# A new instruction order, small guard operations on other engines, and four loads in flight instead of eight in a fused attention and soft-MoE kernel

## The chip, the cores and the metric

One core of one Trainium2 chip runs the whole program. The metric is the device time of one execution in microseconds (us). Five engines work beside each other, each on its own queue in order: PE (TensorE, with its weight loads shown as PEld), DVE (VectorE), ACT (ScalarE), POOL (GpSimd) and SP (SyncE, which issues all DMAs here). They wait for one another by semaphores.

## The reference

Two attentions in a row (32 packed queries over 576 rows, then 576 queries over the 32 packed rows), and a soft mixture of experts over all 4608 rows of the result:

```python
def sm_attn(qq, kk, vv):
    s = scale * np.matmul(qq, kk.transpose(0, 1, 3, 2))
    a = np.exp(s - np.max(s, axis=-1, keepdims=True))
    a = a / (np.sum(a, axis=-1, keepdims=True) + 1e-09)
    return np.matmul(a, vv)
p_packed = sm_attn(p, k, v)                 # 8 batches, 8 heads, 32 x 64
out = sm_attn(q, p_packed, p_packed)        # 8 batches, 8 heads, 576 x 64
...
logits = x @ phi                            # x: 4608 x 512, phi: 512 x 32
d = softmax over the 4608 rows of logits    # per slot, 1e-09 in its sum too
slot_input = d.T @ x                        # 32 slots
h = np.maximum(slot_input[e] @ w1[e], 0.0)  # 8 experts, 4 slots each
slot_out[e] = h @ w2[e]
c = softmax over the 32 slots of logits
return c @ slot_out
```

All data are float32. w1 and w2 together are 33.6 MB, and q, k and v 28.3 MB.

## The kernel before

**Steps.** The attention runs in 8 steps i of 2 batches and 4 heads each; two steps make a round dd (0 to 3). A step's parts have short names, and each is one Python function `f_<name>`: `kt` transposes k on DVE (L393), `s1` scores the packed queries (PE, L409), `mx1`/`e1` the row maxima (DVE, L422) and the exponentials with their row sums `rz` (ACT, L425), `ap`/`apc` transpose them (PE, L442, and a copy), `m` multiplies by v (PE, L464), `rz` (L474) adds the guard 1e-9 to the sums, inverts them and multiplies them by the 0/1 mask `rm` (three DVE instructions, L476, L477, L479), `ppa`/`pp` scale the products with that (ACT L488, DVE L493), `pt`/`ptc` transpose them, `mp`/`mm` multiply by phi. For the second attention `qp`/`qc` transpose q (PE L555, and a copy), `s2` scores (PE, L581), `mx2`/`sb`/`e2` subtract the maxima and take exponentials (DVE L602 and L612, ACT L641), `z2` sums (POOL as a tree, L649 to L655, or DVE, L646), `rc` adds the guard (DVE, L659) and inverts (L660), `n2` normalises (POOL or DVE, L664), `a2p`/`a2c` transpose the result (PE L673). Per round, `lg` makes the logits (PE L697), `f1` to `f6` take the running maximum over all rows and the exponentials (`f3`: three or four DVE instructions, L714 to L723; `f4`: PE, L731 and L739), and `gr`, `rt`, `gt`, `rb`, `gs`, `sa` accumulate the slots' inputs (PE L801, L823, L860). `f_w` (L833) multiplies a tile of ones into a PSUM bank that nobody reads.

**What sets the order.** `ORDER` is a string of such tokens, worked off from left to right: `qp.1.4@6` is part 4 of `qp` in step 1 into PSUM bank 6, and `:a`, `:v`, `:p` name the engine of a copy. Each engine gets its instructions in this order. Matmuls in float32 show in the trace as two records each.

**Loads.** All loads are issued by SP in the order of the list `loads`: p, and then k, q and v of each step, in pieces of 590 KB, then the weights in 33 chunks, of 1 MB but for two halves. They go into one ring in SBUF; `pump` issues the next load in program order once `release` has freed its place (for q and v after their last PE use, for k after its DVE transposes). The framework gives the loads 8 semaphores in turn, so each load also waits for the one eight places ahead. `PLACE` says of the first 21 weight chunks which go to the ring (`r`), which into work tiles that come free late (`0` to `5`, opened by the tokens `late`), and which into the tile a2 (`x`, opened by `lx`).

**After the steps.** The last `gs.3` and one DVE addition (L1012) complete the slots' inputs. Then PE consumes the weight chunks (`layer1a`, L948, 16 chunks of w1; then layer 2, L1002 and L1054), the last 12 loads following into the ring as chunks of w1 are consumed, and at the end the rows of the output are made (L1114), copied and stored.

Of the kernel before, what the change touches and what calls it, by code (L numbers as in the profile page):

```python
# [24 lines left out]
ppa.0.1 ppa.0.0 pp.0.1 kt.1.2 kt.1.3 s1.1.0@4 pp.0.0 kt.1.1 pt.0.0 ptc.0.1:v s1.1.1 ptc.0.0:v mp.0.0
mx1.1.0 mm.0.0:a s2.0.0@0 e1.1.1 s2.0.1 e1.1.0 rz.1.0 kt.2.0 ap.1.0@7 qp.1.4@6 ap.1.2@5 qc.1.4:a
apc.1.0:v qp.1.1@4 qp.1.3@3 apc.1.2:a mx2.0.2 qp.1.0@7 qc.1.1:a qc.1.3:a qp.1.2@6 qc.1.0:a qp.1.5@3
kt.2.3 qc.1.2:a ap.1.1@4 qc.1.5:a kt.2.2 m.1.0@6 apc.1.1:v sb.0.2 m.1.1 m.1.2 kt.2.1 e2.0.0 s1.2.0@0
ppa.1.0 s1.2.1 z2.0.0:p ppa.1.1 pp.1.0 pp.1.1 pt.1.0 mx1.2.0 ptc.1.1:a ptc.1.0:a mp.1.0 kt.3.1
e1.2.0 kt.3.0 mm.1.0:a e1.2.1 s2.1.0@5 rc.0.0 rz.2.0 n2.0.0:p s2.1.1 kt.3.2 kt.3.3 qp.2.2@0 qp.2.1@1  # L30
mx2.1.2 qp.2.5@2 qc.2.1:a qp.2.4@3 ap.2.0@1 qc.2.5:a ap.2.2@4 qc.2.2:v apc.2.0:a qp.2.3@2 qc.2.4:v
qp.2.0@1 sb.1.2 qc.2.3:a a2p.0.1@0 qc.2.0:a ap.2.1@3 a2p.0.0@2 a2c.0.1:a apc.2.1:v e2.1.0 m.2.0@5
apc.2.2:v m.2.1 a2c.0.0:a z2.1.0:p m.2.2 s1.3.0@0 ppa.2.0 ppa.2.1 pp.2.0 pp.2.1 pt.2.0 a2p.0.2@4
kt.4.0 ptc.2.1:a s1.3.1 ptc.2.0:a a2c.0.2:a kt.4.2 rc.1.0 lg.0.0@4 kt.4.3 mp.2.0 n2.1.0:p mm.2.0:a
mx1.3.0 s2.2.0@5 s2.2.1 kt.4.1 e1.3.0 e1.3.1 mx2.2.2 qp.3.1@3 sb.2.2 ap.3.1@2 qc.3.1:a ap.3.2@1
apc.3.1:a qp.3.5@0 a2p.1.1@2 apc.3.2:v qc.3.5:a qp.3.4@3 qp.3.0@7 rz.3.0 qc.3.4:a a2c.1.1:a qp.3.2@0
e2.2.0 ap.3.0@3 qp.3.3@2 apc.3.0:v a2p.1.0@1 qc.3.0:a z2.2.0:v m.3.0@5 a2c.1.0:a qc.3.2:a m.3.1
rc.2.0 m.3.2 qc.3.3:v n2.2.0:p a2p.1.2@7 ppa.3.1 ppa.3.0 pp.3.1 s1.4.0@0 pp.3.0 a2c.1.2:v s1.4.1
kt.5.2 a2p.2.0@7 kt.5.0 lg.0.1 a2c.2.0:v pt.3.0 f1.0.0 a2p.2.1@7 ptc.3.0:a kt.5.3 ptc.3.1:a f2.0.0
a2c.2.1:a mp.3.0 f3.0.0 a2p.2.2@7 mm.3.0:a mx1.4.0 a2c.2.2:a f4.0.0 f5.0.0 s2.3.0@5 fd.0.0 e1.4.1  # L40
kt.5.1 s2.3.1 e1.4.0 f6.0.0 mx2.3.2 ap.4.0@3 ap.4.2@2 ap.4.1@1 apc.4.2:a qp.4.2@0 sb.3.2 apc.4.1:a
qp.4.1@2 qc.4.1:a qp.4.3@1 qp.4.4@2 qc.4.3:a fl.0.0 gr.0.0@5 qc.4.2:v e2.3.0 gz.0.0 apc.4.0:v
qc.4.4:a lg.1.0@7 rt.0.1:v rt.0.0:a z2.3.0:p rz.4.0 s1.5.0@0 gt.0.0 s1.5.1 kt.6.2 rb.0.0 mx1.5.0
gs.0.0 qp.4.0@4 sa.0.0 e1.5.0 qc.4.0:v m.4.0@5 kt.6.1 e1.5.1 m.4.1 rc.3.0 m.4.2 n2.3.0:v ap.5.1@0
ppa.4.1 ap.5.0@1 ppa.4.0 ap.5.2@2 apc.5.1:v apc.5.0:a a2p.3.2@3 apc.5.2:a pp.4.1 a2p.3.1@4 a2c.3.2:v
a2p.3.0@0 a2c.3.1:a m.5.0@1 kt.6.0 a2c.3.0:a kt.6.3 m.5.1 pp.4.0 m.5.2 rz.5.0 pt.4.0 ppa.5.1 lg.1.1
ppa.5.0 pp.5.1 ptc.4.1:a pp.5.0 ptc.4.0:a qp.4.5@0 f1.1.0 pt.5.0 qc.4.5:a f2.1.0 mp.4.0 ptc.5.1:v
ptc.5.0:a f3.1.0 mm.4.0:a mp.5.0 mm.5.0:v f4.1.0 s1.6.0@0 f5.1.0 s1.6.1 kt.7.0 fd.1.0 s2.4.0@4
mx1.6.0 s2.4.1 kt.7.2 e1.6.1 f6.1.0 mx2.4.2 e1.6.0 ap.6.1@3 rz.6.0 qp.5.0@2 apc.6.1:v qp.5.2@1
qc.5.0:a gz.1.0 ap.6.0@0 qc.5.2:a sb.4.2 qp.5.1@2 ap.6.2@3 apc.6.0:a qp.5.4@1 qc.5.1:a qp.5.3@0  # L50
qc.5.4:a apc.6.2:a fl.1.0 gr.1.0@1 e2.4.0 kt.7.3 kt.7.1 qc.5.3:a z2.4.0:p s1.7.0@4 rt.1.1:v rt.1.0:a
gt.1.0 s1.7.1 late.0.0 late.1.0 rb.1.0 gs.1.0 mx1.7.0 qp.5.5@0 qc.5.5:a sa.1.0 rc.4.0 e1.7.1 m.6.0@2
n2.4.0:p m.6.1 e1.7.0 m.6.2 rz.7.0 ap.7.0@7 ppa.6.0 s2.5.0@4 ppa.6.1 apc.7.0:a pp.6.0 pp.6.1
a2p.4.1@7 a2p.4.0@0 a2c.4.1:v pt.6.0 a2c.4.0:a s2.5.1 ptc.6.1:v ptc.6.0:a qp.6.2@7 mx2.5.2 mp.6.0
qc.6.2:a qp.6.5@0 mm.6.0:a qp.6.0@1 qc.6.5:a sb.5.2 qp.6.1@2 qp.6.3@3 qc.6.0:a qp.6.4@0 ap.7.1@7
qc.6.1:a qc.6.3:a a2p.4.2@1 qc.6.4:v ap.7.2@2 e2.5.0 s2.6.0@3 apc.7.2:v a2c.4.2:a z2.5.0:p s2.6.1
apc.7.1:a qp.7.3@7 mx2.6.2 qp.7.1@6 qp.7.2@2 qc.7.3:a qp.7.4@1 lg.2.0@0 qc.7.1:a qc.7.2:a sb.6.2
m.7.0@6 qc.7.4:a m.7.1 late.2.0 rc.5.0 e2.6.0 m.7.2 n2.5.0:v qp.7.5@5 ppa.7.1 ppa.7.0 qp.7.0@4
qc.7.5:a pp.7.1 a2p.5.0@3 pp.7.0 qc.7.0:v pt.7.0 a2c.5.0:a a2p.5.2@5 ptc.7.1:a ptc.7.0:v a2p.5.1@1
z2.6.0:v s2.7.0@2 a2c.5.1:a s2.7.1 late.3.0 rc.6.0 a2c.5.2:v n2.6.0:p mp.7.0 mx2.7.2 lg.2.1 mm.7.0:a  # L60
# [1093 lines left out]
```

## Time and profile before

| | |
|---|---|
| device time, median of 3 runs | 215.29 us (215.11 to 216.77) |
| the profiled execution's own time | 214.82 us |
| its span, first to last instruction | 212.9 us |
| PE busy (2769 matmul records) | 174.0 us, 82% |
| DVE busy | 135.4 us, 64% |
| ACT busy | 82.0 us, 39% |
| POOL busy | 34.9 us, 16% |
| mean granted clock of TensorE | 0.917 of full speed |
| HBM traffic | 62.46 MB read, 9.44 MB written |
| chain that ended last, by engine | PE 41%, DVE 20%, DMA 13%, ACT 11%, issue 4%, POOL 2% |

The times of the trace count from the span's start. A granted clock of 1.00 is 2.4 GHz and 0.50 is 1.2 GHz; a value between them is a stretch that had both. The chain is followed back from the last instruction: at each step to what released it, or to the instruction before it on its engine.

### The profile page before, as it was taken

Reading aid. Unit: us, or ns where it says so; the run is one execution under the profiler, and the core shown is the slowest. Engines: PE = TensorE matmul, PEld = TensorE weight load, DVE = VectorE, ACT = ScalarE, POOL = GpSimd, SP = SyncE. Lnnn points to the kernel's source line nnn. Section 1 sums busy time; section 2 is a strip of 40 time slices with the busy share of each in tenths; the row PEclk is TensorE's granted clock in tenths of the full one; section 3 lists DMA queues with packets and bytes.
Section 4 is the critical chain, followed back from the end, with each engine's and each line's share of the span. In section 5 each row is a group of like instructions: output and inputs, shape, how many; then the busy total and the mean of one; then the engine's idle time right before and its main releaser. Section 6 shows DMA issues by size and latency. Waiting matters only on the chain.

```text
span 212.9 us, 6428 instructions
## 1 busy us (share of the span) xinstructions
PE 174.0 (82%) x2769; PEld 114.2 (54%) x2769; DVE 135.4 (64%) x267; ACT 82.0 (39%) x199; POOL 34.9 (16%) x60
## 2 busy tenths in 40 slices
...
GB/s 212 398 375 366 393 388 394 385 388 390 388 390 388 389 404 376 77 353 192 52 402 416 402 403 425 417 271 197 117 376 428 423 420 393 19 230 408 414 414 306
DMA packets 23195, 72.29 MB, mean 340 GB/s; under 512 B 2176, under 2 KB 2944, under 8 KB 21248
## 3 DMA queue, kind: packets, MB, share of 16 engines
...
HBM read 62.46 MB, written 9.44 MB: 338 GB/s over the span
## 4 chain that ended last, share of the span: by engine, by line
PE 41%; DVE 20%; DMA 13%; ACT 11%; issue 4%; POOL 2%; SPq 1%; ACTq 0%; DVEq 0%
DMA ring<-in_moe_w_dram 9%; PE ps L464 6%; PE ps L948 6%; PE ps L581 5%; DVE work L393 4%; DMA ring<-in_q_dram 3%; PE ps L673 3%; DVE mx L602 3%; PE ps L442 3%; ACT ring L343 3%; ACT work L425 3%; PE ps L555 3%; PE ps L801 3%; PE ps L409 3%; PE ps L823 2%
## 5 line engine op out<-in xcount | busy, mean ns | idle before, releaser
L343 ACT COPY work<-ps 128x512 f32<-128x512 f32 (+3 forms) x65 | 27.8, 466 | 32.0 <-PE ps L555 19.1
L393 DVE STREAM_TRANSPOSE work<-ring 128x576 f32<-128x576 f32 x32 | 23.3, 753 | 3.0 <-DMA ring<-in_k_dram 1.9
L555 PE MATMUL ps<-ident,ring 128*128 128x128 f32 x144 | 20.8, 280 | 1.2 <-DVE a L612 0.9
L581 PE MATMUL ps<-work 128*64 128x64 f32 x576 | 20.8, 235 | 0.5 <-DVE work L347 0.4
L464 PE MATMUL ps<-ring,work 64*64 64x128 f32 x576 | 19.7, 285 | 1.5 <-DVE S_run L873 0.7
L581 PEld LDWEIGHTS ps<-work 128*64 128x64 f32 x576 | 19.5, 149 | 1.9 <-issue 1.1
L464 PEld LDWEIGHTS ps<-ring,work 64*64 64x64 f32 x576 | 17.1, 141 | 4.6 <-ACT work L343 1.6
L555 PEld LDWEIGHTS ps<-ident,ring 128*128 128x128 f32 x144 | 15.8, 141 | 4.3 <-issue 1.1
L347 DVE COPY work<-ps 128x384 f32<-128x384 f32 (+3 forms) x27 | 14.4, 544 | 5.1 <-PE ps L442 2.7
L649 POOL TENSOR_TENSOR zt<-work 128x576 f32<-128x576 f32 x4 | 5.7, 1421 | 63.4 <-ACT work L641 63.4
L409 PE MATMUL ps<-work 32*32 32x288 f32 x512 | 14.5, 430 | 1.8 <-ACT work L343 1.2
L948 PE MATMUL ps<-ring,a2Tb 128*32 128x512 f32 x96 | 14.8, 696 | 0.4 <-DVE a2Tb L1012 0.4
L425 ACT ACTIVATE work<-ps,nm 128x576 f32<-128x576 f32 x16 | 11.7, 738 | 7.8 <-DVE nm L422 7.7
L442 PE MATMUL ps<-ident,work 128*128 128x128 f32 x72 | 11.1, 279 | 2.7 <-ACT work L425 1.7
L602 DVE TENSOR_REDUCE mx<-ps 128x36 f32<-128x1152 f32 x8 | 10.8, 1351 | 3.8 <-PE ps L581 2.6
L422 DVE TENSOR_REDUCE nm<-ps 128x2 f32<-128x1152 f32 x8 | 10.7, 1342 | 2.5 <-PE ps L409 2.5
L347 DVE COPY a2Tb<-ps 128x384 f32<-128x384 f32 (+2 forms) x10 | 5.3, 543 | 10.3 <-PE ps L905 8.8
L343 ACT COPY a2Tb<-ps 128x384 f32<-128x384 f32 x17 | 8.1, 480 | 7.8 <-PE ps L673 7.8
L343 ACT COPY ring<-ps 128x512 f32<-128x512 f32 (+1 forms) x21 | 10.4, 621 | 1.1 <-PE ps L1114 0.6
L347 DVE COPY ring<-ps 128x512 f32<-128x512 f32 (+1 forms) x16 | 9.5, 666 | 1.8 <-PE ps L1106 1.2
L442 PEld LDWEIGHTS ps<-ident,work 128*128 128x128 f32 x72 | 8.1, 142 | 3.8 <-ACT work L425 2.1
L1002 PE MATMUL ps<-ring,hT 128*32 128x512 f32 x88 | 10.1, 593 | 0.0
(140 smaller groups left out, 265.4 us busy)
## 6 DMA issues: line engine op xcount, KB each, us to landing
...
ring<-in_k_dram SPq DMA_DIRECT2D x16, 576.0 KB, 11.9
ring<-in_q_dram SPq DMA_DIRECT2D x16, 576.0 KB, 12.0
ring<-in_v_dram SPq DMA_DIRECT2D x16, 576.0 KB, 12.0
...
```

The costliest lines, as they stand in the source:

```text
L343: nc.scalar.copy(dst, src)
L347: nc.vector.tensor_copy(dst, src)
L393: nc.vector.transpose(kT[:, b2, :, c].rearrange("p m (t r) -> p m t r", t=T), view(f"k{i}.{b2}").rearrange("p (m t c d) -> p m t c d", m=2 ...
L409: nc.tensor.matmul(ps[32 * y : 32 * y + 32, banks["s1", i] + z, 0 : 32 * T], pT[rs, dd, b2, g, c, m], kT[rs, b2, m, c], start=(c == 0), st ...
L422: nc.vector.tensor_reduce(nms[i % 2], s1v(i), axis=AX.XY, op=ALU.max, negate=True)
L425: nc.scalar.activation(a1[:, :, x].rearrange("p t (h r) -> p h t r", h=2), s1v(i)[:, x].rearrange("p h (t r) -> p h t r", t=T), AF.Exp, bi ...
L442: nc.tensor.transpose(ps[:, bank, o : o + P], a1[:, t].rearrange("p x r -> p (x r)"), ident)
L464: nc.tensor.matmul(ps[64 * b2 : 64 * b2 + 64, b + x, 0:P].rearrange("p (m d) -> p m d", m=2), a1T[rs, t, b2], view(f"v{i}.{b2}").rearrange ...
L555: nc.tensor.transpose(ps[:, bank, o : o + P], view(f"q{i}.{b2}")[:, P * n : P * n + P], ident)
L581: nc.tensor.matmul(psf[64 * b2 : 64 * b2 + 64, o + 64 * n : o + 64 * n + 64].rearrange("p (a s) -> p a s", a=2), qT[:, b2, n, 64 * x : 64 ...
L602: nc.vector.tensor_reduce(mxs[i % 2][:, a0:a1].rearrange("p a t -> p (a t)"), s2v(i, j).rearrange("p a t s -> p (a t) s"), axis=AX.X, op=A ...
L948: nc.tensor.matmul(ps[32 * a : 32 * a + 32, b + nh, :], xzf[:, (4 * e + a) * NSLOT : (4 * e + a + 1) * NSLOT], wv[:, j, nh * 512 : (nh + 1 ...
```

## The change

Four things are changed. **The order**: all of `ORDER` is another one, with other engines for some copies and with seven more `w` tokens (`w.4`, 512 columns, four times; `w.3`, 384 columns, three times). `PLACE` puts nine instead of six weight chunks into the ring ahead of the first work tile. **The guards**: DVE's `rz` keeps only its reciprocal; a new part `ra` writes the sums plus a bias on ACT, where the bias is 1e-9 on the rows and columns that are wanted and 3e38 where the mask was 0 (its reciprocal is 0). Where POOL makes the sums of `z2`, POOL adds the guard too, and `rc` doesn't. **The running maximum**: `f2` has PE write the old maximum beside the new transposed one, `f3` is one DVE maximum over both, and `f4` spreads it on PE by four small matmuls and takes the difference by two. **The loads**: of the loads 24 to 55 in the list (v of step 2 up to v of step 7) each waits until the load four places ahead has landed.

```diff
+FEW = range(24, 56)
+AHEAD = 4
-PLACE = "rrrrrr01rrrrrr2rr345x"
+PLACE = "rrrrrrrrr01rrrr2r345x"
...
+    def begin(dst, src):
+        ins = nc.sync.dma_start(out=dst, in_=src).ins
+        if len(begun) in FEW:
+            tc.add_manual_dep(
+                ins,
+                begun[-AHEAD].name,
+                mybir.DependencyInfo(mybir.DependencyClass.Sync, mybir.DependencyReason.DATA),
+                reason="few loads at a time",
+            )
+        begun.append(ins)
...
-    nc.gpsimd.memset(rm, 0.0)
+    nc.gpsimd.memset(rm, FAR)
...
-        nc.gpsimd.memset(rm[32 * c : 32 * c + 32, 1 - c % 2 : 2 - c % 2], 1.0)
+        nc.gpsimd.memset(rm[32 * c : 32 * c + 32, 1 - c % 2 : 2 - c % 2], EPS)
...
+    def f_ra(i, j, bank, eng):
+        for m in range(2):
+            nc.scalar.activation(
+                rzms[i % 2][:, m], rzs[i % 2], AF.Identity, bias=rm[:, m : m + 1], scale=1.0
+            )
     def f_rz(i, j, bank, eng):
-        rz = rzs[i % 2]
-        nc.vector.tensor_scalar_add(rz, rz, EPS)
+        rz = rzms[i % 2].rearrange("p m x -> p (m x)")
         nc.vector.reciprocal(rz, rz)
-        nc.vector.tensor_tensor(
-            rzms[i % 2],
-            rz.unsqueeze(2).broadcast_to([P, 2, 2]),
-            rm.unsqueeze(1).broadcast_to([P, 2, 2]),
-            op=ALU.mult,
-        )
...
         nc.gpsimd.tensor_tensor(z, y[:, :, :, 0], y[:, :, :, 1], op=ALU.add)
+        nc.gpsimd.tensor_scalar_add(z, z, EPS)
+        guarded.add((i, c))
     def f_rc(i, c, bank, eng):
         z = part(zss[i % 2], c)
-        nc.vector.tensor_scalar_add(z, z, EPS)
+        if (i, c) not in guarded:
+            nc.vector.tensor_scalar_add(z, z, EPS)
         nc.vector.reciprocal(z, z)
...
     def f_f3(dd, j, bank, eng):
-        src = ps[0:1, banks["f", dd], W : W + P].rearrange("p (c s) -> p s c", c=4)
-        nc.vector.tensor_reduce(mr, src, axis=AX.X, op=ALU.max)
...
+        n = 4 if dd == 0 else 5
+        src = ps[0:1, banks["f", dd], W : W + n * NSLOT].rearrange("p (c s) -> p s c", c=n)
+        nc.vector.tensor_reduce(m_run[dd % 2], src, axis=AX.X, op=ALU.max)
```

On PE, in steps 0 and 1, the order before has these rows (L442 is `ap.0`, L464 `m.0`, L369 `px.1`, L409 `s1.1`, L506 `pt.0`, L528 `mp.0`, L581 `s2.0`):

```order
L442 MATMUL ps<-ident,work 128x128 x9
L464 MATMUL ps<-ring,work 64x128 x24
L369 MATMUL ps<-a_1_118 64x384 x8
L464 MATMUL ps<-ring,work 64x128 x12
L409 MATMUL ps<-work 32x288 x16
L506 MATMUL ps<-ident,pp_152 128x128 x2
L409 MATMUL ps<-work 32x288 x16
L528 MATMUL ps<-phi_sb,work 64x32 x4
L581 MATMUL ps<-work 64x64 x36
```

The changed kernel has there (its lines are L460, L482, L387, L427, L523, L545 and L598 for the same parts, and L861 for `w`):

```order
L460 MATMUL ps<-ident,work 128x128 x9
L861 MATMUL ps<-ones 128x384
L482 MATMUL ps<-ring,work 64x128 x24
L387 MATMUL ps<-a_1_118 64x384 x8
L482 MATMUL ps<-ring,work 64x128 x12
L861 MATMUL ps<-ones 128x512
L427 MATMUL ps<-work 32x288 x16
L523 MATMUL ps<-ident,pp_155 128x128 x2
L427 MATMUL ps<-work 32x288 x16
L545 MATMUL ps<-phi_sb,work 64x32 x4
L861 MATMUL ps<-ones 128x512
L598 MATMUL ps<-work 64x64 x36
```

Three multiplications of ones now stand ahead of `m.0`, of `s1.1` and of `s2.0`; the rest keeps its order.

On DVE, in step 2, the order before has these rows (`rz.2`'s last two instructions, then two `kt` of step 3, `mx2.1`, two copies and `sb.1`):

```order
L477 RECIPROCAL rz_167<-rz_167 128x2
L479 TENSOR_TENSOR rzm_169<-rz_167,rm 128x4
L393 STREAM_TRANSPOSE work<-ring 128x2x288 x2
L602 TENSOR_REDUCE mx_172<-ps 128x36
L347 COPY work<-ps 128x512
L347 COPY work<-ps 128x128
L612 TENSOR_TENSOR work<-ps,mx_172 128x4x9x32
```

The changed kernel has, for the same step, this from `rz.2` on (L501; then two `a2c` copies, both `pp.2`, `mx1.3`, and `rc.1`'s reciprocal, L680):

```order
L501 RECIPROCAL rzm_172<-rzm_172 128x4
L364 COPY a2Tb<-ps 128x384 x2
L510 SCALAR_TENSOR_TENSOR pp_157<-ps,rzm_172,pt_154 128x128 x2
L440 TENSOR_REDUCE nm_169<-ps 128x2
L680 RECIPROCAL zs_177<-zs_177 128x36
```

The instruction of two SBUF operands behind the reciprocal is gone, and the reciprocal of step 2 stands later, behind `mx2.1` and `sb.1`.

On PE, at the end of the steps, the order before has these rows (L823 is `gt.2`, L709 `f2.3`, L860 `gs.2`, L731 and L739 `f4.3`, L770 `f6.3`):

```order
L823 MATMUL ps<-rep,rt 128x32 x4
L709 MATMUL ps<-ident,nml 1x128
L860 MATMUL ps<-rb,pp_152 64x64 x2
L860 MATMUL ps<-rb,pp_153 64x64 x2
L731 MATMUL ps<-ones,m_179 128x1
L739 MATMUL ps<-dm,ones 128x32
L770 MATMUL ps<-rw,ones 128x32
```

and the changed kernel (L851 is `gt.2`, L730 and L737 `f2.3`, L888 `gs.2`, L752 and L761 `f4.3`, L861 `w`, L798 `f6.3`):

```order
L851 MATMUL ps<-rep,rt 128x32 x4
L730 MATMUL ps<-m_run_146,ones 1x32
L737 MATMUL ps<-ident,nml 1x128
L888 MATMUL ps<-rb,pp_155 64x64 x2
L888 MATMUL ps<-rb,pp_156 64x64 x2
L752 MATMUL ps<-ones,m_run_147 32x1 x4
L761 MATMUL ps<-m_run_146,ones 128x32
L761 MATMUL ps<-m_run_147,less 128x32
L861 MATMUL ps<-ones 128x512
L798 MATMUL ps<-rw,ones 128x32
```

The small matmuls of the running maximum are four more here, and a `w` of 512 columns stands between them and `f6.3`; a `w` of 384 columns stands behind `gr.3`, and two more stand in the round before (one ahead of `a2p.6`, one behind `f4.2`).

## Rows read from the trace of the kernel before

**Rows 1.** Stretches: start:end us, length, busy us (records) of PE, PEld, DVE, ACT, POOL; PE clock, DMA share, GB/s
```profile
10.00:127.00 117.00, 104.21 (x2118) 80.69 (x2118) 92.30 (x170) 59.86 (x149) 25.14 (x30) 0.96 0.94 351
20.00:30.00 10.00, 9.73 (x153) 7.63 (x154) 7.04 (x14) 3.54 (x11) 0.00 (x0) 0.66 1.05 393
45.00:50.00 5.00, 4.87 (x109) 3.72 (x107) 1.84 (x6) 2.05 (x4) 3.10 (x5) 0.70 1.06 392
127.00:145.00 18.00, 13.03 (x164) 8.06 (x160) 13.94 (x35) 5.88 (x18) 2.78 (x2) 0.87 0.84 345
145.00:150.00 5.00, 3.35 (x20) 2.51 (x24) 1.73 (x5) 0.56 (x2) 1.12 (x1) 0.50 0.59 213
```

**Rows 2.** Loads: SP's issues (start, us), the chain (start, us), and issue to landing of L140
```profile
151.20 13.93 SPq L140 DMA_DIRECT2D ring<-in_moe_w_dram  x12
162.45 18.53 DMA ring<-in_moe_w_dram
DMA to landing us min/median/max: 2.1/11.9/18.6
```

**Rows 3.** Order of time on POOL and on DVE: start us, us, instruction
```profile
38.44 2.13 POOL L664 TENSOR_TENSOR work<-work,zs 128x1152 f32<-128x1152 f32 x1 [0.71 <-DVE rz L476]
38.62 1.97 DVE L479 TENSOR_TENSOR rzm<-rz,rm 128x4 f32<-128x4 f32 x1
121.28 1.36 DVE L664 TENSOR_TENSOR work<-work,zs 128x1152 f32<-128x1152 f32 x1
```

**Rows 4.** Groups of instructions by line: busy us, mean ns of one, idle before them
```profile
L477 DVE RECIPROCAL rz<-rz 128x2 f32<-128x2 f32 x8 | 1.3, 166 | 0.3
L476 DVE TENSOR_SCALAR rz<-rz 128x2 f32<-128x2 f32 x8 | 3.6, 449 | 2.7 <-ACT work L425 2.7
L479 DVE TENSOR_TENSOR rzm<-rz,rm 128x4 f32<-128x4 f32 x8 | 3.6, 448 | 0.3
L659 DVE TENSOR_SCALAR zs<-zs 128x36 f32<-128x36 f32 x8 | 1.7, 218 | 0.3 <-POOL zs L655 0.2
L655 POOL TENSOR_TENSOR zs<-zt 128x36 f32<-128x36 f32 x5 | 1.2, 246 | 0.4
L347 DVE COPY a2Tb<-ps 128x384 f32<-128x384 f32 x8 | 4.3, 540 | 1.9 <-PE ps L673 1.6 <-PE ps L905 0.3
L719 DVE TENSOR_TENSOR m<-mr,m_run 1x128 f32<-1x128 f32 x3 | 0.8, 279 | 0.1
L488 ACT ACTIVATE pt<-ps,rzm 128x64 f32<-128x64 f32 x16 | 4.2, 312 | 6.8 <-PE ps L464 5.5 <-issue 1.2
```

**Rows 5.** Order of time on PE: start us, us, instruction, [idle before it <- whom it waited for]
```profile
18.84 0.72 PE L409 MATMUL ps<-work 32*32 32x288 f32 x16 [1.21 <-ACT work L343]
...
23.36 4.09 PE L581 MATMUL ps<-work 128*64 128x64 f32 x72
...
43.92 0.52 PE L673 MATMUL ps<-ident,work 128*128 128x128 f32 x3 [2.06 <-DVE work L347]
...
45.40 3.43 PE L464 MATMUL ps<-ring,work 64*64 64x128 f32 x72
...
60.25 2.20 PE L464 MATMUL ps<-ring,work 64*64 64x128 f32 x72
...
68.06 2.32 PE L581 MATMUL ps<-work 128*64 128x64 f32 x72
...
128.85 0.87 PE L673 MATMUL ps<-ident,a 128*128 128x128 f32 x6 [1.04 <-POOL a L664]
...
142.74 0.41 PE L770 MATMUL ps<-rw,ones 128*128 128x32 f32 x2 [1.38 <-ACT al L755]
...
145.61 1.92 PE L823 MATMUL ps<-rep,rt 128*128 128x32 f32 x8 [0.76 <-ACT rt L343]
...
149.26 7.62 PE L948 MATMUL ps<-ring,a2Tb 128*32 128x512 f32 x48 [0.45 <-DVE a2Tb L1012]
...
182.03 0.70 PE L833 MATMUL ps<-ones 128*128 128x256 f32 x2
```

More of the change, by code (lines that the diff above doesn't have):

```diff
@@ L25 @@
[L25 to L60, printed above, removed]
@@ new lines @@
+ptc.0.0:v mp.0.0 mx1.1.0 w.4.0@3 mm.0.0:v e1.1.0 s2.0.0@0 e1.1.1 s2.0.1 ra.1.0 rz.1.0 ap.1.0@7
+mx2.0.2 qp.1.5@6 apc.1.0:a qp.1.4@5 qp.1.3@4 qc.1.5:a qp.1.1@7 ap.1.2@3 sb.0.2 qc.1.1:a ap.1.1@6
+apc.1.2:a qp.1.2@7 apc.1.1:a qp.1.0@3 qc.1.2:a qc.1.3:v m.1.0@0 e2.0.0 kt.2.1 m.1.1 qc.1.4:v
+qc.1.0:a kt.2.2 m.1.2 z2.0.0:p kt.2.0 ppa.1.0 ppa.1.1 pp.1.0 s1.2.0@4 pp.1.1 kt.2.3 pt.1.0 ptc.1.0:a
+s1.2.1 ptc.1.1:a mp.1.0 mx1.2.0 mm.1.0:a s2.1.0@0 rc.0.0 e1.2.0 s2.1.1 n2.0.0:p kt.3.1 e1.2.1 kt.3.0
+qp.2.3@3 ra.2.0 ap.2.1@7 mx2.1.2 qc.2.3:a qp.2.4@6 qp.2.0@5 apc.2.1:a a2p.0.0@4 qc.2.0:a qp.2.2@3
```

105 lines of the change are left out of this document (72 added, 33 removed).

## The prediction

> **What bounds the kernel now.** I read the chain of waits first, then the table of stretches, then PE, DVE and POOL in order of time where the chain changes engine, and last the loads.
>
> The end hangs on one moment. When the slots' inputs are complete, PE starts on the weights at 149.26 [rows 5]; only then do chunks of the ring come free, and SP issues the last twelve loads from 151.20 on [rows 2]. The last piece of the chain in which a load is waited for ends at 162.45 + 18.53 = 180.98 us [rows 2], and the remaining 31.9 us of the span are layer 2's last chunk, the output rows and their stores. None of that changes. So the span is the start of the weights plus 212.9 - 149.3 = 63.6 us, and what the change is worth is what it takes out of the stretch before 149.3. Earlier loads don't matter as long as the 21 chunks that have a place are there by then.
>
> In that stretch PE is the busiest engine but not alone: from 10 to 127 us it is busy 104.2 of 117 us, DVE 92.3, ACT 59.9 [rows 1]. PE idles 12.8 us there and in three places runs at the lower clock: granted 0.66 from 20 to 30 us, 0.70 from 45 to 50, and 0.87 and then 0.50 from 127 to 150 [rows 1]. Before the second fall PE had stood idle for 2.06 us on a DVE copy, before the first it had idled 1.21 us on ACT [rows 5]. What the lower clock costs is seen on equal work: 72 records of `s2` take 4.09 us at 23 us and 2.32 at 68; 72 of `m` take 3.43 at 45 us and 2.20 at 60 [rows 5].
>
> **Term 1, the start (10 to 30 us).** Time lost to the clock is (1 - 0.66) x 10 = 3.4 us, as PE is busy 9.73 of the 10 [rows 1]; 1.8 of it are the `s2` above. Three `w` now stand there. A `w` of 256 columns takes 0.70 us at full clock [rows 5]; by columns 512 take 1.40 and 384 take 1.05. The one ahead of `s1.1` fits into the wait of 1.21 us [rows 5] but for 0.2; the one ahead of `m.0` I charge in full, and the one ahead of `s2.0` too, where the row shows no wait: 0.2 + 1.05 + 1.4 = 2.6. If they hold the clock, the term is -3.4 + 2.6 = **-0.8**; if they don't, +2.6; if they all fall into waits, -3.4.
>
> **Term 2, step 2 (38 to 50 us).** DVE's last `rz` instruction, on 128x4 elements, took 1.97 us, from 38.62 to 40.59; POOL's `n2.0` ran from 38.44 to 40.57 [rows 3]. Undisturbed such instructions are as short as the reciprocal's 0.17; the means of 0.45 for L476 and L479 [rows 4] show that this happens again elsewhere. Two DVE `kt`, `mx2.1` and two copies stood behind it, and PE's 2.06 us of idle time at 43.92 is for the second of these copies. The instruction is gone; so are L476 and the guard L659 (0.22 [rows 4]) ahead of it: 1.97 + 0.16 + 0.22 = 2.35 us off the chain. POOL adds the guard itself: one more instruction, at least nothing and at most about the 0.25 of L655 [rows 4], and I take 0.25, its nearest row. That leaves -2.1. With PE fed, the clock's loss behind it, (1 - 0.70) x 5 = 1.5 us [rows 1], can go as well: -3.6 at best, 0 if another DVE instruction is late instead. The order there is another one (the reciprocal stands behind `mx2.1`), so I take two thirds: **-2.4**.
>
> **Term 3, the middle (50 to 127 us).** Clock 1.00 nearly throughout, so only waits can go. DVE loses: the rest of L476 and L479, 3.6 + 3.6 - 2.1 = 5.1 us; the guard L659 in most steps, 0.9; one instruction of `f3` per round, 0.28 [rows 4]; and `n2.5`, 1.36 us, which stood in the chain [rows 3] and goes to POOL. That is 7.7. By the tokens DVE takes over 14 copies from ACT and gives back 5; nine at no more than 0.54 [rows 4] are 4.9, and as most are shorter than this row I take half, 2.4. Net -5.3. How much of it was in the way? DVE makes up 20% of the chain, 42.6 us, of 107 us busy up to 149: 40%. So **-2.1**, between 0 (PE is the bound, 89% busy) and -5.3.
>
> **Term 4, the end of the steps (127 to 151 us).** The rounds' last parts are a thin chain here, and PE is cold in it: (1 - 0.87) x 13.03 = 1.7 and (1 - 0.50) x 3.35 = 1.7 us lost [rows 1]. The first weight chunk runs cold too: the first load follows 1.94 us after L948's start [rows 2, 5], and at full clock about half, -0.9. `f3` is shorter by L719's 0.28; `f4`'s four more small matmuls run on parts of the array and I cost them at 0, hidden in the wait of ACT behind them, and at most 0.3. Four `w` pay for the clock: two of 1.4 us stand in waits of 1.04 and 1.38, one of 1.05 in 0.76 [rows 5], and the last in several short ones, of which I charge half: 1.2. Sum -1.7 - 1.7 - 0.9 - 0.3 + 1.2 = -3.4. The clock may fall again in the waits that stay, so 80%: **-2.7**; without the clock, +0.9.
>
> **Term 5, ACT.** Each step adds two `ra` on ACT. Bounds for one: nothing, and the 0.31 of L488, which has 64 columns and also an operand per row [rows 4]; I take 0.3, as it is the nearest row. 8 x 0.6 = 4.8 us, less the copies given to DVE, 2.4: ACT is busy 2.4 us more. It was busy 51% [rows 1]; its share of the chain, 11% or 23 us of 82, makes **+0.7**, from 0 to 2.4.
> The Trainium skill speaks against this part (ScalarE: Activation LUTs, Rules for kernel authors): an addition belongs on VectorE, not on ScalarE. Going by that rule, the pair costs ACT 0.6 us where the two undisturbed DVE instructions cost 0.33, so +0.27 x 8 = 2.2 us and no gain from the move. The rows of step 2 differ: there one of the DVE instructions took 1.97 us.
>
> **Term 6, loads four places ahead.** Eight loads in flight are 8 x 0.59 MB / 392 GB/s = 12.0 us [rows 1], which is the median of 11.9 from issue to landing, while the shortest is 2.1 [rows 2]. So a load mostly waits in line. Four in flight are 6.0 us of transfer, more than 2.1, and the queue stays fed: I take 0. Nothing but later loads stands behind the waiting issue on SP's queue, and the ring (4.4 steps of k, q, v) keeps them ahead of PE and DVE. A gain is not excluded by a row, but I find none to price. The other end: if landing still took 11.9 us, loads 24 to 55 would run at 198 GB/s, 95 us instead of 48, the 21 chunks (22 MB) would be late by about 25 us, and all with them.
>
> **Sum.** -0.8 - 2.4 - 2.1 - 2.7 + 0.7 = -7.3 us. The profiled execution's own time is 214.82: 207.5. The median of the runs lies 0.5 above it, so **208.0**.
>
> **The rivals.**
> *Only the cold stretches pay.* PE is the bound between them, and DVE's freed time turns into idle time of DVE. For it: PE 89% busy [rows 1]. Against: the 2.06 us of PE idle at 43.92. Terms 1 and 4 alone: 214.82 - 3.5 + 0.5 = 211.8.
> *PE is fed throughout.* Terms 1 to 3 at their best ends and term 4 in full, -3.4 - 3.6 - 5.3 - 3.4 + 0.7 = -15.0: 200.3; half way from the forecast to there is 204. Against: the steps still alternate between engines.
> *Nothing is gained.* The waits move to ACT's `ra` and to POOL, which takes over a second long `n2` (2.13 us against 1.36 on DVE), and what the clock gives goes to the `w`: about 214.8. The rule on ScalarE above leads here as well: terms 2 and 3 at 0, +2.2 on ACT, -3.5 from 1 and 4: 214.0.
> *Slower: the `w` stand in PE's way.* Seven are 4 x 1.4 + 3 x 1.05 = 8.75 us. If PE has ready work behind each and the clock falls elsewhere anyway, all of it is added; terms 2 and 3 take back 4.5: 215.3 + 4.3 = 219.6. It decides from the point where less than half of the `w` stand in waits; before, at least three of the seven places had one of about their length [rows 5].
>
> **How the numbers follow.** Forecast (205.5 to 210.5): 50%. Only the cold stretches (210.5 to 213.1): 20%. Fed throughout (below 205.5): 9%. Nothing gained (213.1 to 217.4): 12%. Slower by the `w`, or by slow loads (2%): 9%. Faster by over 1%, which is below 213.1, is 78% (1% is about what a measurement of this kernel can tell from no change), within 1% 13%, slower 9%. The range 203.0 to 214.5 leaves out some 5% below and 14% above.
>
> **What would show it.** The start of the weights (L948's successor, L976) near 142 instead of 149.3, with 63 to 64 us behind it. `s2.0` near 2.3 us and `m.2` near 2.2. No DVE instruction of `rz` or `rc` stretched to the end of a POOL instruction. Granted clock above 0.9 in the 20 us before the weights. Loads of steps 2 to 7 landing some 6 us after issue at about 390 GB/s. The forecast is wrong if PE's idle time in the steps stays near 13 us, or if the clock falls in spite of the `w`.

## The result, and the profile after

The changed kernel takes 204.1 us (median of 4 runs, 203.9 to 207.0) against 215.2 us of the kernel before, a ratio of 0.952 with a 95% interval of 0.942 to 0.962. That is 11 us less, where 7.3 us less were forecast. Times here and below are medians of all runs, while a ratio leaves out runs that are over 1.5% above the fastest of the same kernel, so the two need not agree. The profiled execution took 206.97 us, of which 205.2 are its span; the same kernel run again for the experiments left a profile of 203.14 us (span 201.4), and where the two differ both are shown.

The stretches of the changed kernel, with the columns of [rows 1] (start:end, length, busy time of PE, PEld, DVE, ACT and POOL, granted clock, DMA share, GB/s):

```profile
10.00:127.00 117.00, 108.17 (x2218) 82.14 (x2216) 90.72 (x161) 64.30 (x166) 31.58 (x37) 1.00 1.01 374
20.00:30.00 10.00, 9.48 (x196) 7.59 (x195) 7.20 (x12) 5.72 (x14) 0.00 (x0) 1.00 1.04 390
45.00:50.00 5.00, 4.35 (x115) 2.94 (x93) 4.49 (x8) 2.94 (x9) 3.36 (x5) 1.00 1.02 371
127.00:142.00 15.00, 12.29 (x122) 8.02 (x126) 7.45 (x23) 2.96 (x10) 0.65 (x1) 0.77 0.76 299
```

The two falls of the clock at 20 and at 45 us are gone (0.66 and 0.70 before). The one ahead of the weights is not: 0.77 in this execution (0.87 and then 0.50 before). PE in order of time (start, us, instruction, idle time before it and whom it waited for):

```profile
22.88 2.08 PE L598 MATMUL ps<-work 128*64 128x64 f32 x63
...
37.72 0.60 PE L572 MATMUL ps<-ident,ring 128*128 128x128 f32 x4 [1.57 <-issue]
...
41.88 2.20 PE L482 MATMUL ps<-ring,work 64*64 64x128 f32 x72
...
50.47 0.45 PE L598 MATMUL ps<-work 128*64 128x64 f32 x7 [1.11 <-issue]
...
127.94 1.20 PE L693 MATMUL ps<-ident,a 128*128 128x128 f32 x9 [1.17 <-DVE a L684]
...
141.73 5.77 PE L976 MATMUL ps<-ring,a2Tb 128*32 128x512 f32 x50 [0.45 <-DVE a2Tb L1040]
```

Step 2's `m` takes 2.20 us where it took 3.43, and the wait of 2.06 us for a DVE copy ahead of it [rows 5] is gone. The weights (L976) begin at 141.73 instead of 149.26, and 205.2 - 141.73 = 63.5 us lie behind them, as before. So in this execution the whole gain lies ahead of the weights. What has grown is the releaser "issue" on PE: time in which PE waited for nothing that the profile shows. It is 3.9 us in this execution (0.26, 0.26, 1.57, 1.11 and 0.68); on PE before it was 1.2.

The groups that the guards touch (busy us, mean ns, idle before), of ACT, DVE and POOL; the counterparts are in [rows 4]:

```profile
L495 ACT ACTIVATE rzm<-rz,rm 128x2 f32<-128x2 f32 x16 | 3.9, 291 | 0.2
L501 DVE RECIPROCAL rzm<-rzm 128x4 f32<-128x4 f32 x8 | 1.3, 157 | 2.0 <-ACT rzm L495 2.0
L673 POOL TENSOR_SCALAR zs<-zs 128x36 f32<-128x36 f32 x5 | 1.5, 300 | 0.4
```

`ra` costs ACT 0.29 us each, and the reciprocal of `rz` is never stretched. One guard still is. In step 7 DVE makes the sums, so the guard of `rc.7` stays on DVE, and it runs beside a memset on POOL:

```profile
125.06 0.98 POOL L948 MEMSET a2Tb<- 128x1056 f32 x1 [3.67 <-PE ps L717]
125.08 1.00 DVE L679 TENSOR_SCALAR zs<-zs 128x36 f32<-128x36 f32 x1
```

At 109.08 us the same instruction takes 0.18 us. Behind it on DVE stand `rc.7`'s reciprocal and `n2.7`, for which PE waits 1.17 us at 127.94. (Before, this guard took 0.57 us.) Last, the loads (KB each, median us from issue to landing) and SP's issue of the last twelve:

```profile
ring<-in_k_dram SPq DMA_DIRECT2D x16, 576.0 KB, 6.0
ring<-in_q_dram SPq DMA_DIRECT2D x16, 576.0 KB, 7.0
ring<-in_v_dram SPq DMA_DIRECT2D x16, 576.0 KB, 6.8
```

```profile
142.80 14.43 SPq L142 DMA_DIRECT2D ring<-in_moe_w_dram  x12
```

Four loads in flight land after 6.0 to 7.0 us, against the 11.9 us of [rows 2], and SP follows 1.07 us behind the start of the weights instead of 1.94.

### The profile page after: what moved, and what is told of

The parts are those of the page before. It is cut to its first block, busy times and chain, and to the rows that moved or that the text cites. A ratio compares the mean times of both kernels' runs of the same rounds, so it can differ in the third digit from the quotient of the medians.

```text
span 205.2 us, 6513 instructions
## 1 busy us (share of the span) xinstructions
PE 172.7 (84%) x2819; PEld 112.7 (55%) x2819; DVE 127.1 (62%) x243; ACT 83.0 (40%) x206; POOL 38.7 (19%) x67
## 4 chain that ended last, share of the span: by engine, by line
PE 55%; DVE 16%; ACT 7%; DMA 6%; issue 5%; SPq 2%; POOL 1%; ACTq 0%; DVEq 0%; POOLq 0%
PE ps L598 8%; PE ps L1030 6%; PE ps L572 6%; PE ps L427 5%; DMA ring<-in_p_dram 5%; PE ps L482 4%; PE ps L693 4%; ACT ring L360 3%; PE ps L460 3%; PE ps L861 3%; PE ps L829 2%; DVE work L411 2%; PE ps L717 2%; PE ps L851 2%; PE ps L976 2%
## 5 line engine op out<-in xcount | busy, mean ns | idle before, releaser
L598 PE MATMUL ps<-work 128*64 128x64 f32 x576 | 19.5, 224 | 1.7 <-issue 1.4
L598 PEld LDWEIGHTS ps<-work 128*64 128x64 f32 x576 | 18.0, 138 | 4.2 <-issue 3.0
L482 PE MATMUL ps<-ring,work 64*64 64x128 f32 x576 | 18.0, 272 | 0.0
L482 PEld LDWEIGHTS ps<-ring,work 64*64 64x64 f32 x576 | 15.8, 133 | 2.6 <-issue 1.9
L861 PE MATMUL ps<-ones 128*128 128x512 f32 (+3 forms) x28 | 15.7, 668 | 1.1 <-DVE ones L117 1.1
L364 DVE COPY work<-ps 128x512 f32<-128x512 f32 (+3 forms) x29 | 14.2, 498 | 3.4 <-PE ps L460 1.4
L684 POOL TENSOR_TENSOR work<-work,zs 128x1152 f32<-128x1152 f32 x4 | 8.5, 2132 | 35.7 <-PE ps L888 23.0
L427 PE MATMUL ps<-work 32*32 32x288 f32 x512 | 13.9, 412 | 1.3 <-issue 0.7
L976 PE MATMUL ps<-ring,a2Tb 128*32 128x512 f32 x104 | 12.9, 594 | 0.4 <-DVE a2Tb L1040 0.4
L364 DVE COPY a2Tb<-ps 128x384 f32<-128x384 f32 (+2 forms) x14 | 7.5, 550 | 9.3 <-PE ps L933 8.8
L460 PE MATMUL ps<-ident,work 128*128 128x128 f32 x72 | 11.3, 279 | 1.4 <-ACT work L443 1.2
L460 PEld LDWEIGHTS ps<-ident,work 128*128 128x128 f32 x72 | 8.0, 140 | 2.9 <-ACT work L443 1.4
```

The lines of the kernel that those rows point to most:

```text
L364: nc.vector.tensor_copy(dst, src)
L427: nc.tensor.matmul(ps[32 * y : 32 * y + 32, banks["s1", i] + z, 0 : 32 * T], pT[rs, dd, b2, g, c, m], kT[rs, b2, m, c], start=(c == 0), st ...
L460: nc.tensor.transpose(ps[:, bank, o : o + P], a1[:, t].rearrange("p x r -> p (x r)"), ident)
L482: nc.tensor.matmul(ps[64 * b2 : 64 * b2 + 64, b + x, 0:P].rearrange("p (m d) -> p m d", m=2), a1T[rs, t, b2], view(f"v{i}.{b2}").rearrange ...
L598: nc.tensor.matmul(psf[64 * b2 : 64 * b2 + 64, o + 64 * n : o + 64 * n + 64].rearrange("p (a s) -> p a s", a=2), qT[:, b2, n, 64 * x : 64 ...
L861: nc.tensor.matmul(ps[:, bank, 0 : P * n].rearrange("p (n c) -> p n c", n=n), ones, ones.unsqueeze(1).broadcast_to([P, n, P]), start=True, ...
```

## Experiments

Two theories stood against each other when the result was known. Theory 1: the forecast's terms hold, and some of them are larger than priced (the guards on DVE, the clock at the end). Theory 2: the missing 4 us are in the loads, priced at 0; in the later expectations the name stands for what the runs had shown by then. The kernels of a group ran on one chip. In the three groups the kernel before took 216.4, 215.1 and 214.7 us (medians).

**The same kernel again** (first and third group, no edit).

> The changed kernel itself, unchanged, for a second profile. Its first profile was of a run of 206.97 us, the other runs took 203.86 to 204.40. In that profile PE stands idle for 1.57, 1.11 and 0.68 us at 36.2, 49.4 and 57.4 us with no semaphore that the trace shows ("issue"). Theory 1 (these idle times are chance and are the whole difference between the runs): a profile of a run near 204 shows less than 1 us of them in all, and the weights start (L976) near 138.7 instead of 141.73. Theory 2 (they belong to the kernel and the difference lies elsewhere): they are there again, 3 us or more.

> The changed kernel itself, beside the three others on this chip. It should stand at 204 to 205 us, a ratio of 0.935 to 0.952 to the kernel before, and its idle time of PE that waits for nothing visible between 2.5 and 4 us.

205.0 us (202.1 to 209.9), ratio 0.935 (0.924 to 0.946); and 205.2 us (202.1 to 206.1), ratio 0.951 (0.944 to 0.957). One kernel thus spreads over 4 us and more, and the two profiles show where. First the one of 203.14 us, then the one of 206.14, PE ahead of the weights:

```profile
125.94 1.20 PE L693 MATMUL ps<-ident,a 128*128 128x128 f32 x9 [1.18 <-DVE a L684]
...
128.33 1.08 PE L851 MATMUL ps<-rep,rt 128*128 128x32 f32 x8
...
131.03 1.13 PE L861 MATMUL ps<-ones 128*128 128x512 f32 x2
...
138.81 4.52 PE L976 MATMUL ps<-ring,a2Tb 128*32 128x512 f32 x40 [0.45 <-DVE a2Tb L1040]
```

```profile
126.82 1.20 PE L693 MATMUL ps<-ident,a 128*128 128x128 f32 x9 [1.18 <-DVE a L684]
...
129.48 1.92 PE L851 MATMUL ps<-rep,rt 128*128 128x32 f32 x8
...
133.74 2.08 PE L861 MATMUL ps<-ones 128*128 128x512 f32 x2
...
141.81 1.51 PE L976 MATMUL ps<-ring,a2Tb 128*32 128x512 f32 x12 [0.45 <-DVE a2Tb L1040]
```

Both idle for 1.18 us on the same DVE instruction. In the second the clock falls soon after it: the eight matmuls of L851 take 1.92 us instead of 1.08 and the `w` 2.08 instead of 1.13. Of the 3.0 us by which its weights start later, 0.9 were there at L693 and 2.1 came behind it. In the first the clock falls too, but later and for less long: its granted clock is 0.90 from 120 to 136 us and 0.97 from 136 to 141, where the second has 0.78 and 0.69. So in none of the three profiles of the changed kernel do the four `w` at the end hold the clock up to the weights. "Issue" on PE is 2.5 us in the first profile, between what the two theories wanted, and 2.7 in the second. So it belongs to the kernel, and its amount changes from one execution to the next: from 3.9 to 2.5 us it makes 1.4 of the 2.9 us between the starts of the weights at 141.73 and 138.81. With such a spread a difference of less than about 2 us between two kernels is not shown by medians.

**Eight loads in flight again** (first group). In the changed kernel:

```diff
-FEW = range(24, 56)
+FEW = range(0)
```

> The changed kernel with eight loads in flight again: no load waits for the one four places ahead. Theory 1 (loads only wait in line, term 6 of the prediction at 0): 204 us as the changed kernel, within 0.7, loads of steps 2 to 7 landing 12 us after issue. Theory 2 (PE's idle times without a visible wait are its own instructions that arrive late behind the queued loads, and four in flight shorten that): 206 to 209 us, with more than 4 us of such idle time on PE between 20 and 80 us.

208.7 us (206.6 to 210.2), ratio 0.960 (0.946 to 0.975): 3.7 us more than the changed kernel beside it (5.5 by the ratios, 0.960 against 0.935). Loads take 12 us to land again. PE, in order of time:

```profile
25.36 0.46 PE L598 MATMUL ps<-work 128*64 128x64 f32 x9 [0.77 <-issue]
37.86 0.60 PE L572 MATMUL ps<-ident,ring 128*128 128x128 f32 x4 [1.57 <-issue]
50.33 0.45 PE L598 MATMUL ps<-work 128*64 128x64 f32 x7 [0.85 <-issue]
58.72 1.46 PE L427 MATMUL ps<-work 32*32 32x288 f32 x47 [1.50 <-issue]
64.92 0.68 PE L598 MATMUL ps<-work 128*64 128x64 f32 x15 [0.66 <-issue]
```

With 0.26 at 21 us this is 5.6 us of "issue" against 2.5 in the profile of the changed kernel beside it: 3.1 of the 3.5 us by which the weights start later (142.34 against 138.81). The stretch from 56 to 57 us has one packet on the queue that brings the engines their instructions (packets, MB, share of 16 engines):

```profile
q8 instruction: 1, 0.02, 6.5%
```

There is one such packet of 16 KB ahead of the end of each of the five gaps above (in the stretches that begin at 22, 35, 47, 56 and 62 us), and they move over the same 16 DMA engines as the loads. Three more packets, at 29, 41 and 68 us, have no gap behind them. My reading is that PE outruns its instructions, and that they come late when eight loads stand in line. Two things in the traces speak for the first half of it. Each of the five gaps ends 2.35 to 2.56 us behind the start of its packet, and so it is, within 2.3 to 2.7 us, with every "issue" gap of PE that ends later than 22 us in the ten profiles of the new order with four, six or eight loads in flight (35 gaps). And between the ends of these five gaps PE shows 508, 510, 253 and 256 records (matmuls and weight loads), each time close to 256 or twice 256: the gaps stand at equal distances in the program. For the second half, take the time from PE's passing of such a place to the start of the next packet, for the packets between 33 and 72 us: in the new order its median is about 3.8 us with eight and with six loads in flight, 2.5 to 3.9 in the profiles with four and 1.1 with two. That the gaps shrink with fewer loads is shown; that a packet waits behind the loads is the likeliest reading and not shown, since the trace has its transfer and not its request.

**The four-ahead rule alone, in the kernel before** (first group): only `begin` and its two constants are added.

> The kernel before with the loads 24 to 55 each waiting for the load four places ahead, nothing else changed. Theory 1 (nothing from the loads): 215 us, within 1. Theory 2 (the shorter queue frees PE of late instructions): 211 to 213 us, if the old order has as many such idle times; its profile shows only about 1.2 us of them on PE (0.19 at 54.9 and 0.98 at 96.4), so by that at most 1.2 us.

215.4 us, ratio 0.991 (0.987 to 0.996): about 1 to 2 us. The rule is worth less there than in the new order. In the old order PE idled only 1.2 us by "issue" with eight loads, so there was less to gain. The profile of this run took 217.5 us, the longest of its ten, and has 3.1 us of it: 1.75 and 0.16 us with no packet 2.3 to 2.7 us ahead of their ends, and 0.77 and 0.42 with one. The latter are again 1.2 us, so the idle time shows no gain here, and where the 1 to 2 us come from stays open.

**Without the seven `w`** (first group): the seven new `w` tokens are taken out of ORDER.

> The changed kernel without its seven added multiplications of ones (the five at the very start stay). Theory 1 (they hold the clock, terms 1 and 4 of the prediction, worth 3.5 us net): 207 to 208 us, granted clock below 0.8 between 20 and 30 us and s2.0 near 4 us instead of 2.3. Theory 2 (the clock is held by the better fed PE, the ones only fill waits or stand in the way): 203 to 204.5 us, clock 1.00 from 20 to 120 us all the same.

207.1 us (205.9 to 207.6), ratio 0.955 (0.947 to 0.963): 2.1 us more than the changed kernel beside it (4.3 by the ratios, whose intervals just don't meet). Its stretches:

```profile
20.00:30.00 10.00, 8.77 (x207) 7.76 (x211) 7.40 (x13) 6.22 (x14) 0.50 (x1) 1.00 1.05 389
120.00:136.00 16.00, 13.68 (x138) 8.79 (x144) 10.55 (x26) 5.20 (x15) 0.98 (x1) 0.63 0.90 370
136.00:141.00 5.00, 3.61 (x48) 2.73 (x32) 1.21 (x4) 0.65 (x2) 0.00 (x0) 0.50 0.55 185
```

At the start the clock is 1.00 without any added `w`. At the end it is 0.63 and 0.50, where the changed kernel beside it has 0.90 and 0.97. The weights start at 141.46, 2.65 us later, and their first fifty matmuls take 7.39 us instead of 5.77. So theory 2 holds for the start and theory 1 for the end. But the end alone doesn't tell the two kernels apart: from the nine transposes of `a2p.7` (L693) to the weights it takes 15.0 us here, and 12.9, 13.8 and 15.0 us in the three profiles of the changed kernel.

**Without the first three `w`** (second and third group): the tokens `w.3` ahead of `m.0`, `w.4` ahead of `s1.1` and `w.4` ahead of `s2.0` are taken out.

> The changed kernel without the first three added w (ahead of m.0, s1.1 and s2.0); the four at the end stay. As term 1 had it (the w hold the clock there): the granted clock falls again between 20 and 30 us and the time rises by 0.8 us. Theory 2 (the run without any added w showed a clock of 1.00 from 10 to 120 us: the order keeps PE busy and the three only cost): clock 1.00, and the time falls by up to their 2.6 us; if they stand in waits, 0. So 0.94 to 0.95 to the kernel before against 0.933 to 0.945.

> The changed kernel without the first three added w, once more and beside the changed kernel itself. Theory 2 (the first three w only cost, the clock stays at 1.00 there without them): 1.5 to 2.6 us less than the changed kernel. Rival (they stand in waits, and 201.9 us was that chip): the same time.

201.9 us (200.6 to 203.7) in the second group, but 205.9 us (201.9 to 207.0) beside the changed kernel's 205.2 in the third. No difference is shown. The clock is 1.00 from 10 to 120 us in both profiles. Both even keep it up to the weights, at 137.41 and 136.94 us, which no profile of the changed kernel does; but the run with six loads below, also without the three, doesn't keep it either, so this is no proof against them. PE's row `s2.0` ends at the same time with and without them, since its last matmuls wait for "issue": the first row is of the third group's run without the three, the second of the changed kernel beside it.

```profile
25.18 0.33 PE L582 MATMUL ps<-work 128*64 128x64 f32 x3 [1.09 <-issue]
```

```profile
24.98 0.46 PE L598 MATMUL ps<-work 128*64 128x64 f32 x9 [0.39 <-issue]
```

**The guards back on DVE** (second group), new order, `w` and loads kept; the mask `rm` is 0 and 1 again:

```diff
     def f_ra(i, j, bank, eng):
-        for m in range(2):
-            nc.scalar.activation(
...
+        return
...
     def f_rz(i, j, bank, eng):
-        rz = rzms[i % 2].rearrange("p m x -> p (m x)")
+        rz = rzs[i % 2]
+        nc.vector.tensor_scalar_add(rz, rz, EPS)
         nc.vector.reciprocal(rz, rz)
+        nc.vector.tensor_tensor(
+            rzms[i % 2],
...
-        nc.gpsimd.tensor_scalar_add(z, z, EPS)
-        guarded.add((i, c))
```

> The changed kernel with the guards back on VectorE: rz is three DVE instructions again, rc adds its guard on DVE, ra issues nothing, and POOL's z2 adds no guard. Order, w and loads stay. Theory 1 (the forecast's terms 2, 3 and 5: the DVE instructions are in the way, stretched while POOL works): 2.4 us of step 2 come back, and 40% of the 5.1 + 0.9 us of the middle, 2.4; ACT's 16 additions go, which gives back up to 0.7; so about 4.1 us over the changed kernel, a ratio of 0.97 to the kernel before, and DVE instructions of rz of over 1 us in the trace. Rival (PE is the bound, the freed DVE time was idle time): no difference or 0.7 us less, a ratio of 0.94 to 0.95.

205.0 us (201.6 to 208.5). The changed kernel itself did not run in this group. It took 205.0 and 205.2 us in the two others, but the kernel without the first three `w`, of which no cost is shown, took 201.9 us in this one. So by medians the guards on ACT and POOL are worth between 0 and 3 us here. In the profile (202.93 us) the weights start at 138.35, and DVE is busy 97.5 us from 10 to 127 instead of 92.4. The stretched instruction is still there, as DVE's rows show, and PE waits behind it:

```profile
41.70 1.20 DVE L498 TENSOR_SCALAR rz<-rz 128x2 f32<-128x2 f32 x1
42.94 0.17 DVE L499 RECIPROCAL rz<-rz 128x2 f32<-128x2 f32 x1
43.14 0.63 DVE L500 TENSOR_TENSOR rzm<-rz,rm 128x4 f32<-128x4 f32 x1
```

```profile
45.02 0.59 PE L527 MATMUL ps<-ident,pp 128*128 128x128 f32 x2 [0.51 <-DVE pp L514]
...
125.55 1.20 PE L695 MATMUL ps<-ident,a 128*128 128x128 f32 x9 [0.25 <-DVE a L686]
```

This is `rz.2`. In the new order it stands behind `mx2.1` and `sb.1`, and PE's wait behind it is 0.51 us, where the old order had 2.06. That the weights start no later than in the changed kernel is in part luck: here the guard of `rc.7` ended (123.68) just before POOL's memset began (123.69), and PE waits 0.25 us at `a2p.7` instead of 1.18. What is shown is that the 2.4 us of step 2 don't come back; that the move is worth nothing in the new order is not.

**The guards moved, in the old order** (second group): `ra`, `rz`, `z2`, `rc` and the mask of the changed kernel in the kernel before, `ra.i` behind the later `e1` of each step.

> The kernel before with only the guards moved: ra on ACT stands behind each step's last e1, POOL's z2 adds its own guard, DVE keeps the two reciprocals. Old order, old w, eight loads in flight. Theory 1 (guards in the way in the old order as well): 2.4 + 2.4 - 0.7 = 4.1 us less than the kernel before, a ratio of 0.98, and the 1.97 us instruction of step 2 gone. Rival (the gain lies in the order by the clock's periods, the guards only allow it): within 1 us of the kernel before.

211.9 us (210.8 to 212.7), ratio 0.987 (0.982 to 0.992): 3 us less. Step 2's DVE and PE:

```profile
38.32 0.15 DVE L470 RECIPROCAL rzm<-rzm 128x4 f32<-128x4 f32 x1
```

```profile
41.79 0.52 PE L662 MATMUL ps<-ident,work 128*128 128x128 f32 x3
...
43.16 2.20 PE L451 MATMUL ps<-ring,work 64*64 64x128 f32 x72 [0.20 <-DVE work L598]
```

The instruction of 1.97 us [rows 3] is gone, the wait of 2.06 us ahead of the transposes at 43.92 (L673, here L662 at 41.79) is no longer there, `m.2` runs at full clock, and the weights start at 146.22, 3.0 us earlier. So the mechanism of step 2 is real, and the new order removes most of it by itself (0.51 us of wait, above).

**The order alone** (third group): guards on DVE, no added `w`, eight loads in flight.

> The changed kernel's order alone: guards on VectorE, none of the seven added w, eight loads in flight as before. Theory 2 (the parts add up, as the runs so far price them: guards 0 in this order, the first three w -2.5, the last four +3.5 to +5, four in flight +3.7): 204.5 - 2.5 + 4.5 + 3.7 = 210.2 us, a ratio of 0.976, with a clock of 1.00 up to 120 us. Rival (the order needs the guards or the loads to gain): 213 to 216, as much as the kernel before.

210.6 us (209.4 to 211.2), ratio 0.982 (0.979 to 0.986), 4.1 us less than the kernel before and 5.5 more than the changed kernel beside it, with a clock of 1.00 from 20 to 30 us. The sum of the expectation was 210.2. The first stretch of [rows 1] in its profile:

```profile
10.00:127.00 117.00, 104.82 (x2173) 80.82 (x2171) 94.61 (x178) 60.99 (x147) 29.06 (x31) 0.99 1.02 381
```

In it PE's waits for other engines are about 7 us, where they were about 11, and the clock is 0.99, where it was 0.96; but "issue" on PE has grown from 1.2 to 5.1 us. This run keeps the new running maximum and the new `PLACE`; neither was tried alone, so the 4.1 us are of these and the order together.

**Two loads in flight** (second group): `AHEAD = 2` in the changed kernel.

> The changed kernel with a load issued when the one two places ahead has landed, in place of four. Theory 2 (a long line of loads makes PE's own instructions late: idle time of PE that waits for nothing else was 2.5 to 3.9 us in the changed kernel and 5.6 with eight loads in flight): that idle time falls to 1 to 2 us, and the time by 1 to 2 us. Rival (that idle time has nothing to do with the loads): it stays at 2.5 us or more, the time does not fall. Loads land about 3.5 us after issue; if the queue runs dry between them they move some 320 GB/s in place of 390, which the 4.4 steps that the ring is ahead should hide; if not, PE waits for loads and the time rises.

229.6 us, ratio 1.070 (1.065 to 1.075). Landing and PE's longest wait in the steps:

```profile
ring<-in_q_dram SPq DMA_DIRECT2D x16, 576.0 KB, 5.0
```

```profile
61.51 1.11 PE L572 MATMUL ps<-ident,ring 128*128 128x128 f32 x4 [5.22 <-DVE work L364]
```

Two loads in flight land after 5.0 us, not 3.5, which is 2 x 0.59 MB / 5.0 us = 236 GB/s. DVE waits 19.5 us for loads, and the first weights are asked for at 107 us instead of 76 (profile of 203.14 us). My expectation missed this: the ring's lead was used up. It can't tell anything about PE's instructions, as PE was starved otherwise.

**Six loads in flight** (third group): `AHEAD = 6`, without the first three `w`.

> The changed kernel without the first three added w and with a load issued when the one six places ahead has landed, in place of four. Theory 2 (the longer the line of loads, the later PE's own instructions; eight cost 3.7 us over four): half of that, 1 to 2 us over the run without the first three w, landing about 9 us after issue, and more idle time of PE that waits for nothing visible. Rival (eight only lose because SP's queue is full to its end and blocks; six are as good as four): the same time. Rival 2 (four leave gaps between loads, six none): faster by up to 1 us.

207.0 us (205.2 to 209.2), ratio 0.963 (0.958 to 0.968), against 205.9 and 0.946 (0.940 to 0.952) of the same kernel with four. Landing after 9.0 us, and "issue" on PE 5.1 us against 1.7:

```profile
50.40 0.22 PE L582 MATMUL ps<-work 128*64 128x64 f32 x1 [1.18 <-issue]
58.55 1.41 PE L411 MATMUL ps<-work 32*32 32x288 f32 x41 [1.48 <-issue]
```

The gaps stand at nearly the same places in PE's program as with eight. By the medians six cost 1.1 us, less than such runs can tell; by the ratios, whose intervals don't meet, 3.6 us. By "issue", and by the 3.8 us from PE's passing of a place to the next packet, six stands nearer to eight than to four. So the rival that only eight lose is not borne out, and the length of the line is the likelier cause; but part of the 7.3 us between the two profiled runs (209.2 and 201.9 us) is the clock ahead of the weights, which fell here and not there.

## Why the prediction was right, and where its size was off

Right were the direction, the place (all ahead of the weights) and the mark: weights near 142, 63 to 64 us behind them, `s2.0` in about 2.5 us (2.08 and 0.46), `m.2` at 2.20, no stretched reciprocal of `rz`. Two marks were missed. The clock was to be above 0.9 in the 20 us before the weights; it was 0.83 from 122 to 142 us in the first profile, so a clock that falls in spite of the `w`, which I had named as a sign of being wrong, came up at the end. And no DVE instruction of `rc` was to be stretched to the end of one of POOL; the guard of `rc.7` was. The forecast of 207.5 us for a profiled execution stands beside 206.97, but that was the longest of the four runs, so that its weights start near 142 is in part luck (138.81 in the profile of 203.14 us). By the medians 4 us were missing.

**Term 6, the loads, priced at 0, is the step that failed.** It asked only whether the queue would stay fed, and that was right (371 to 390 GB/s in the steps). "A gain is not excluded by a row, but I find none to price" passed over what else moves on the DMA engines. With eight loads in flight the changed kernel is 3.7 us slower, so without this term the change gives 216.4 - 208.7 = 7.7 us, by the side of the forecast's 7.3. That these two agree is in part luck, as the terms below don't agree one by one. The other end that I named, loads as the bound, was met by two in flight.

**Terms 2 and 3, the guards: -4.5 forecast.** Step 2's chain was read rightly, and in the old order the guards' move brings 3 us. In the changed kernel no gain from it is shown, and up to 3 us are not excluded; the order already takes most of the wait out of the way. Term 3's 40% of 5.3 us is not borne out: with 5.1 us more on DVE from 10 to 127 us PE was as busy there as in the changed kernel (109.0 and 108.9 us). The 40% also set DVE's share of the chain over the whole span against its busy time up to 149 us only. (By the tokens 33 copies go to DVE and 24 leave it, not 14 and 5; the net of nine holds. And the chances of the parts below 213.1 add up to 79%, not 78.) There the rival "only the cold stretches pay" was right that PE is the bound. What the terms forecast came, as far as is shown, from the order, 4.1 us with the running maximum and `PLACE`.

**Term 1, the start: -0.8 forecast.** The clock does go to 1.00, but it is the order that holds it, since it holds without the `w` too. They cost nothing that could be measured, so the +2.6 was wrong: at full clock 512 columns take 1.13 us, not 1.40, where 256 took 0.70 [rows 5], so the time doesn't go by the columns alone; and they stand ahead of waits that end at the same time.

**Term 4, the end: -2.7 forecast, -2.1 by the run without `w`.** The size is about right as far as such runs can tell, and so was the doubt that the clock may fall again: in all three profiles of the changed kernel it fell to the lower level ahead of the weights, in one for a short time only. The -0.9 for the first weights was right for the first late load (1.07 us behind the weights instead of 1.94), but the prediction also held the time behind the weights fixed at 63.6 us, and with 63.5 us in the first profile nothing of the 0.9 shows there; in the other two it is 62.6.

**Term 5, ACT: +0.7 forecast.** `ra` was priced rightly at 0.3 us; the run without it, which has the guards on DVE instead, is not faster, so no cost of `ra` shows. Alone it wasn't tried. The Trainium skill (ScalarE: Activation LUTs, Rules for kernel authors) prefers VectorE for an addition. The runs don't bear that out here: in the old order the move of the guards off VectorE, to ACT and POOL, is worth 3 us, and in the new one no loss by it is shown.

**Sum of the runs:** order -4.1, guards 0 (to -3), `w` -2.1, four in flight -3.7, together -9.9 us, beside 9.5 to 11.4 measured in the three pairs with the kernel before. Each of these is a difference of medians, good to about 2 us. The rival slower by the `w` is excluded by the run without them. Still open is why the "issue" gaps end at about 65 us in the new order although the weights' loads then wait 11 us and longer, and why the clock falls at the end in one execution and not in another. No version faster than the changed kernel is shown. The traces point to one that was not tried: with the guard of `rc.7` out of the memset's way, PE's wait at `a2p.7` may be up to 0.9 us shorter.
